# A spectral gate kernel: the last token transform of two row blocks done together on the quarters of the matmul array

## The chip, the cores and the metric

One core of a Trainium2 chip. The metric is the device time of one launch in microseconds (us), the median of the runs. Engines are named as in the profile: PE is the matmul engine (PEld its weight load), DVE the vector engine, ACT the scalar engine, POOL the one that issues the software DMAs, SP the one that issues the hardware DMAs.

## The reference

```python
x = A_x                                        # 1 x 2048 tokens x 512 channels
xn = _layernorm(x, axis=-1)
s = irfft2(rfft2(xn) * (A_w_r + 1j * A_w_i))   # over tokens and channels
h = _layernorm(xn, axis=-1)
u = _gelu(einsum("bsd,sf->bdf", h, B_w1) + B_b1)    # F = 1792
g = _silu((einsum("bdf,fs->bds", u, B_w2) + B_b2).transpose(0, 2, 1))
return x + s * g
```

All data are 32-bit floats. Two branches start from the normalised x: a filter in the two-dimensional frequency domain, and a two-layer network over the tokens whose output gates the filter's result.

## The kernel before

Token t stands at partition t // 16 and in row block j = t % 16, so the 2048 x 512 matrix is 16 row blocks of 128 partitions x 512 channels. The program has three stages.

- **Up to about 100 us**: layer norm of each block, the first products of the network (`hidden_early`), and the first half of the token transform (`first_transform`, `fold`), whose result goes into `ey`, 128 channel pairs x 4 channel groups x 64 frequency columns x 16 blocks x 2.
- **From about 100 to 207 us**: the other network products (`hidden_rest`), gelu, and the filter in eight steps (`filter_pair`), which reads and rewrites `ey`. Two of its matmul groups already run on 64 x 64 quarters of the array: the one that reads `gf` and `sh`, four F32 matmuls with 512 columns each, and the one that reads `xc` and `hf`.
- **From about 207 us to the end**: the second network layer by Strassen-Winograd products, the channel transform back, the last token transform, gate and output. 

In the last stage a loop runs over eight pairs p; a pair is the row blocks j0 = p and j1 = p + 8. Each pair has seven products in the order `ORDER = (1, 2, 5, 6, 3, 7, 4)`; each is 21 matmuls (7 slices of the hidden dimension, each as high x high, high x low, low x high parts; F32R, 128 x 256 columns). Here "product 3" is the one with n = 3. The moving operands are the forms fa, fb, fc, fd of u and the stationary ones are w2f, made for each product by `w2_form`: ACT copies the high part from the loaded weights (L735), DVE subtracts it to get the low part (L736). Three buffers hold w2f, and the form for the product after next is made while PE works. The forms of products 6 and 3 first need a sum of weight blocks (L745 on DVE, `added_up`); each of the sums overwrites the tile `s` that the form before reads, so sum, ACT copy and DVE subtraction follow one another.

Beside the products, each row block j goes through these steps:

- `gathered(j)`: ACT copies block j out of `ey` into `yt` (L807).
- `channels(j, yt)`: four F32 matmuls 128 x 128 (L814; each runs as two passes, so the profile counts eight), then ACT copies one half (L816, `od`), DVE makes sum and difference (L818, L819, `es`) and six more small additions (L821 to L830, `tt` and `y`), and `split` makes a high part `ch` on ACT and a low part `cl` on DVE (L145).
- `spectral(j, y)`: the last token transform, three F32R matmuls of 128 x 512 with the constant `cft` (L148 to L150).
- `gate` (L845, Silu on ACT), `finish` (L853, multiply on DVE) and a DMA. For all blocks but the last the DMA adds into the output, which already holds x (POOL queue, L855); the last block adds x itself (L857) and writes by SP (L858), in two halves of 256 channels.

The products of a pair accumulate in PSUM: products 1, 6, 7 and 4 use the same tile `bx`, and between them ACT or DVE read it (`copied`, `summed`), so product 4 waits until DVE has read `bx` after product 7. In this stage the program orders nothing by hand: the tile scheduler sets the order on each engine, and each engine then runs its queue in that order.

## Time and profile before

| what | value |
|---|---|
| time, median of 3 runs | 380.28 us (380.25 to 381.03) |
| profiled execution: time / span | 380.5 us / 378.7 us |
| granted PE clock, mean | 0.999 |
| PE, DVE, ACT and POOL busy over the span | 98%, 85%, 59%, 20% |
| DMA, last stage (240 to 340 us) | 0.80 to 0.83 of 16 engines busy |

The span is the part of the execution from the first to the last instruction of the program; 1.8 us lie around it. Busy shares are means over stages with different limits, so the prediction reads single stretches of the timeline. In the timeline a row gives the start of the first instruction, the time from there to the end of the last, and how many were merged. Matmuls overlap (one starts while the one before drains), so what a group costs on PE is the distance from its start to the start of the next group, not the second column.

### The profile page before, as it was taken

How to read it: one execution, taken by the hardware profiler on the slowest of the kernel's cores; microseconds unless marked ns; L12 is line 12 of the kernel's file. 1: busy time of each engine (PE TensorE's matmuls, PEld its weight loads, DVE VectorE, ACT ScalarE, POOL GpSimd, SP SyncE). 2: the span in 40 equal slices, each digit the busy share in tenths (PEclk: the TensorE clock that was granted, in tenths of full speed). 3: DMA queues.
4: the chain of work that ended last, by engine and by line, in shares of the span. 5: the costliest groups of instructions: out<-in, count | busy, mean ns of one | idle time of the engine just before them, and what ended most of it. 6: DMA issues, size and time to landing. Idle time of an engine off the chain costs nothing.

```text
span 378.7 us, 7729 instructions
## 1 busy us (share of the span) xinstructions
PE 371.0 (98%) x2872; PEld 326.7 (86%) x2872; DVE 321.6 (85%) x691; ACT 223.7 (59%) x405; POOL 74.5 (20%) x125
## 2 busy tenths in 40 slices
PE   8999999999999999999999899999999999999994
PEld 4888888888877777777888899999999999999994
DVE  5899999985489999999998888897969787987873
ACT  4677867763964444476528685756656465646441
POOL 2133232232222222211111012030302020200100
PEclk9999999999999999999999999999999999999999
DMA  8884778304276475767557289797969696885603
GB/s 257 283 284 147 244 254 275 115 1 126 76 224 216 164 230 188 253 211 234 174 197 158 83 251 212 231 176 198 183 171 222 133 222 133 234 156 153 101 0 55
DMA packets 34101, 68.42 MB, mean 181 GB/s; under 512 B 4352, under 2 KB 17552, under 8 KB 33936
## 3 DMA queue, kind: packets, MB, share of 16 engines
q1 hardware_dynamic: 25712, 43.03, 36.2%
q0 software_dynamic: 8352, 24.91, 29.5%
q8 instruction: 22, 0.36, 0.4%
q14 instruction: 15, 0.12, 0.1%
HBM read 59.53 MB, written 8.13 MB: 179 GB/s over the span
## 4 chain that ended last, share of the span: by engine, by line
PE 86%; DVE 7%; ACT 3%; issue 2%; POOL 0%; DVEq 0%; ACTq 0%; POOLq 0%
PE ps L879 34%; PE ps L134 20%; PE ps L402 20%; PE ps L241 4%; PE ps L814 3%; PE ps L391 2%; PE ps L149 1%; PE ps L148 1%; PE ps L150 1%; ACT w2f L735 1%; DVE w1l L145 1%; DVE fa L307 1%; DVE xc L601 1%; DVE xc L603 1%; DVE w2f L736 1%
## 5 line engine op out<-in xcount | busy, mean ns | idle before, releaser
L402 PE MATMUL ps<-h,w1h 128*128 128x512 f32 x224 | 58.7, 398 | 0.0
L134 PE MATMUL ps<-h,w1h 128*128 128x512 f32 x176 | 56.2, 401 | 0.0
L736 DVE TENSOR_TENSOR w2f<-s,w2f 128x896 fp32r<-128x896 f32 x32 | 34.8, 1092 | 15.6 <-ACT w2f L735 14.9
L402 PEld LDWEIGHTS ps<-h,w1h 128*128 128x128 f32 x224 | 40.9, 188 | 7.9
L879 PE MATMUL ps<-fa,w2f 128*128 128x256 f32 x336 | 43.3, 281 | 0.4 <-DVE w2f L736 0.4
L879 PE MATMUL ps<-fb,w2f 128*128 128x256 f32 x336 | 42.4, 280 | 0.1
L879 PEld LDWEIGHTS ps<-fa,w2f 128*128 128x128 f32 x336 | 41.3, 188 | 1.3 <-DVE w2f L736 0.6
L879 PEld LDWEIGHTS ps<-fb,w2f 128*128 128x128 f32 x336 | 40.5, 188 | 0.7 <-DVE c L849 0.5
L879 PE MATMUL ps<-fc,w2f 128*128 128x256 f32 x336 | 40.9, 279 | 0.0
L134 PEld LDWEIGHTS ps<-h,w1h 128*128 128x128 f32 x176 | 31.6, 188 | 10.7 <-issue 4.9
L879 PEld LDWEIGHTS ps<-fc,w2f 128*128 128x128 f32 x336 | 39.9, 188 | 0.0
L735 ACT ACTIVATE w2f<-s 128x896 fp32r<-128x896 f32 x32 | 30.1, 948 | 15.1 <-DVE s L745 15.1
L726 POOL DMA_DIRECT2D s<-in_w_dram x16 | 14.0, 877 | 108.1 <-DVE es L819 26.8
L134 PE MATMUL ps<-h,w1l 128*128 128x512 f32 x88 | 34.4, 391 | 0.0
L736 DVE TENSOR_TENSOR w2f<-a,w2f 128x896 fp32r<-128x896 f32 x24 | 26.0, 1085 | 5.9 <-ACT w2f L735 5.9
L402 PE MATMUL ps<-h,w1l 128*128 128x512 f32 x112 | 30.6, 389 | 0.0
L735 ACT ACTIVATE w2f<-a 128x896 fp32r<-128x896 f32 x24 | 22.7, 950 | 10.8 <-PE ps L879 7.5
L402 PEld LDWEIGHTS ps<-h,w1l 128*128 128x128 f32 x112 | 21.0, 188 | 4.5
L145 ACT ACTIVATE w1h<-w1s 128x384 fp32r<-128x384 f32 (+1 forms) x26 | 14.6, 566 | 13.8 <-PE ps L134 11.2
L397 DVE TENSOR_TENSOR w1l<-w1r,w1h 128x512 fp32r<-128x512 f32 (+1 forms) x32 | 20.9, 652 | 2.1 <-DMA w1r<-in_w_dram 1.6
L584 POOL DMA_DIRECT2D xc<-xc x16 | 9.8, 619 | 64.3 <-ACT xc L581 54.5
L855 POOL DMA_DIRECT2D out_dram<-g x15 | 13.6, 908 | 43.2 <-DVE g L853 43.2
(119 smaller groups left out, 744.7 us busy)
## 6 DMA issues: line engine op xcount, KB each, us to landing
a<-in_w_dram SPq DMA_DIRECT2D x22, 448.0 KB, 3.8
wt<-in_wk_dram POOLq DMA_DIRECT2D x16, 512.0 KB, 5.4
s<-in_w_dram SPq DMA_DIRECT2D x16, 448.0 KB, 3.8
s<-in_w_dram POOLq DMA_DIRECT2D x16, 448.0 KB, 6.9
w1s<-in_w_dram SPq DMA_DIRECT2D x36, 128.0 KB, 2.6
w1r<-in_w_dram SPq DMA_DIRECT2D x16, 256.0 KB, 3.8
xc<-xc POOLq DMA_DIRECT2D x16, 256.0 KB, 3.0
x<-in_x_dram SPq DMA_DIRECT2D x15, 256.0 KB, 4.3
```

Of the source, the lines that this page charges most:

```text
L134: return lambda *args, **kw: self.keep(operation(*args, **kw))
L145: return A.activation(hi, src, AF.Copy), V.tensor_sub(lo, src, hi.bitcast(F32))
L241: T.matmul(z[:, b], h[:, b * P:(b + 1) * P], c, start=True, stop=True)
L397: keep(V.tensor_sub(dst, src, hi.bitcast(F32)))
L402: T.matmul(ps[:, bank + i], w[wi][:, i * P:(i + 1) * P], hj, start=first and j == 0, stop=last and j == NJ - 1)
L584: keep(G.dma_start(*(v.rearrange("p s t c -> p s (t c)") for v in (there[c::2], here[1 - c::2, ::-1]))))
L726: G.dma_start(t, w2_half(*added), accum_op=ALU.add)
L735: step(A.activation(wf[:, 0], v, AF.Copy))
L736: step(V.tensor_sub(wf[:, 1], v, wf[:, 0].bitcast(F32)))
L814: T.matmul(pe[:, b % 2, b // 2], yt[:, b], ci[:, b], start=True, stop=True)
L855: G.dma_start(out[:, j, cols], g[:, cols], accum_op=ALU.add)
L879: T.matmul(o, wf[:, wi, i], ui, start=m + a == 0 and n in (1, 2, 5), stop=m == NH - 1 and a == 2, skip_group_check=n in (6, 3, 7, 4))
```

## The change

Both row blocks of a pair now go through the channel transform and the last token transform together.

- **Layout.** The symmetry of the last transform is used: a sum and a difference of frequency columns k and 63 - k' are formed in advance, so that even and odd tokens need only 64 of the 128 rows each. `gathered(p)` does it while it copies the pair out of `ey`: two small ACT copies and four DVE additions or subtractions of 240 elements, whose results stand 65 (or 63) elements apart within each pair of values. The tile `yt` has one buffer.
- **`channels(p)`** has the eight F32 matmuls of both blocks; **`unfolded(p)`** has the work behind them on twice the width: one ACT copy of 512 elements, two DVE operations of 512, two of 128, four of 256. The split into `ch` and `cl` is gone.
- **`spectral(p)`**: four F32 matmuls, each 64 x 64 with 512 columns, on the four quarters of the array (rows r, columns e), into PSUM bank e ^ r. They replace the six F32R matmuls of two calls before.
- **Tokens** are permuted: partitions 0 to 63 are the even tokens, 64 to 127 the odd ones. So `w2_form` reads its source with a step of two elements, and the DMAs of xr, b2t and of the output are issued once for each half of the partitions.
- **Order.** Matmuls of the last stage are now held in program order (`T = Kept(...)`, whose line the order shows as L140). `channels(0)` stands behind product 2 of the first pair; `spectral(p)` and `channels(p + 1)` stand between products 7 and 4; for the last pair `spectral` stands behind product 6.
- In the second stage, one ACT copy into `ey` became two; at the start, c_ft is half as large and comes by SP instead of POOL.

```diff
+    b = f.T.reshape(64, 2, P)
+    b = np.concatenate([np.stack([b[0, 0], b[1, 0] + b[1, 1]])[None], b[2:3], b[4:34]]).reshape(64, P)
+    ft = np.concatenate([np.concatenate([b[:, 0::2], b[:, 1::2]], 1)] * 2)
...
-        "c_ft": _parts(f.T, 1),
+        "c_ft": ft.astype(np.float32),
...
-            v = src.rearrange("p (f q) -> p f q", q=P)
-            step(A.activation(wf[:, 0], v, AF.Copy))
-            step(V.tensor_sub(wf[:, 1], v, wf[:, 0].bitcast(F32)))
+            v = src.rearrange("p (f q e) -> p f e q", q=64, e=2)
+            parts = wf.rearrange("p w f (e q) -> p w f e q", e=2)
+            step(A.activation(parts[:, 0], v, AF.Copy))
+            step(V.tensor_sub(parts[:, 1], v, parts[:, 0].bitcast(F32)))
...
+        T = Kept(nc.tensor, keep)
+        halved = (slice(0, 64), slice(0, None, 2)), (slice(64, P), slice(1, None, 2))
...
-        def gathered(j):
-            yt = fp.tile([P, 4, P], F32, name=f"yt{j}", tag="yt", bufs=2)
-            A.activation(yt.rearrange("p b (l c) -> p b l c", c=2), ey[:, :, :, j], AF.Copy)
-            return yt
+        def gathered(p):
+            yt = fp.tile([P, 2, 4, 130], F32, name=f"yt{p}", tag="yt")
+            yts[p] = yt
+            for i, j in enumerate((p, p + NP)):
+                t = yt[:, i]
+                to = t[:, :, :P].rearrange("p b (e s c) -> p b e s c", e=2, c=2)[:, :, ::1 - 2 * i, 0:2]
+                A.activation(to, ey[:, :, 0:4, j].rearrange("p b (e s) c -> p b e s c", e=2), AF.Copy)
+                same = t.rearrange("p b (c t) -> p b t c", c=2)[:, :, 4:64:2]
+                other = t[:, :, 1:127].rearrange("p b (c t) -> p b t c", c=2)[:, :, 4:63:2, ::-1]
+                first, second = (ey[:, :, k, j] for k in (slice(4, 34), slice(63, 33, -1)))
+                yield V.tensor_add((same, other)[i], first, second)
+                yield V.tensor_sub((other, same)[i], first, second)
+
+        def channels(p):
+            yt = yts.pop(p)
+            for i in range(2):
+                pe = ps[:, 6 + i].rearrange("p (h b c) -> p h b c", b=2, c=P)
+                for b in range(4):
+                    T.matmul(pe[:, b % 2, b // 2], yt[:, i, b, :P], ci[:, b], start=True, stop=True)
+
+        def unfolded(p):
+            pe = ps[:, 6:8].rearrange("p i (h k) -> p i h k", h=2)
+            od = fp.tile([P, 2, 256], F32, name=f"od{p}", tag="od")
+            A.activation(od, pe[:, :, 1], AF.Copy)
+            es = fp.tile([P, 2, 2, 2, P], F32, name=f"es{p}", tag="es")
+            V.tensor_add(es[:, :, 0].rearrange("p i b c -> p i (b c)"), pe[:, :, 0], od)
+            V.tensor_sub(es[:, :, 1].rearrange("p i b c -> p i (b c)"), pe[:, :, 0], od)
+            yield
...
+            V.tensor_add(y[:, 0, :, :, 0], ev[:, :, :, 0], ov)
+            V.tensor_sub(y[:, 1, :, :, 0], ev[:, :, :, 0], ov)
+            yield
...
-        def spectral(j, y):
-            mm3(ps[:, j // NP], cft[:, 0], cft[:, 1], *y, True, True)
+        def spectral(p):
+            y = ys.pop(p)
+            for e, cols in enumerate((slice(0, 64), slice(64, P))):
+                for r, rows in enumerate((slice(0, 64), slice(64, P))):
+                    i = e ^ r
+                    T.matmul(ps[cols, i].rearrange("p (s k) -> p s k", s=2), cft[rows, cols], y[rows, :, i], start=True,
+                             stop=True)
...
+            for rows, tokens in halved:
+                if j + 1 < NJ:
+                    G.dma_start(out[tokens, j, cols], g[rows, cols], accum_op=ALU.add)
+                else:
+                    SY.dma_start(out[tokens, j, cols], g[rows, cols])
...
+                    if more:
+                        spectral(p)
+                        run(gathering)
+                        channels(p + 1)
+                        pieces = unfolded(p + 1)
+                        finish(g0, j0, whole)
```

How the built program's order moves, at three places.

First, PE in the middle of the stage: the end of product 7 (the rows that read fb with the first w2f) and the start of product 4 (the next w2f). `ch` and `cl` are the split operand of `spectral`, `yt` is the operand of `channels`, `y` the unsplit operand. Before:

```order
L879 MATMUL ps<-fb_2623,w2f_2_3262 128x256 x3
L148 MATMUL ps<-ch_3308,cft 128x512
L814 MATMUL ps<-cd,yt_3317 128x128
L149 MATMUL ps<-cl_3309,cft 128x512
L150 MATMUL ps<-ch_3308,cft 128x512
L814 MATMUL ps<-cd,yt_3317 128x128 x3
L879 MATMUL ps<-fb_1443,w2f_2_3312 128x256 x3
```

With the change:

```order
L140 MATMUL ps<-fb_2607,w2f_3_3469 128x256 x3
L140 MATMUL ps<-fb_2625,w2f_3_3469 128x256 x3
L140 MATMUL ps<-y_3396,cft 64x512 x4
L140 MATMUL ps<-cd,yt_3399 128x128 x8
L140 MATMUL ps<-fb_1444,w2f_3_3499 128x256 x3
```

Both blocks' channel matmuls and the quarters stand here now; the second `spectral` (behind product 1) and the second `channels` (behind product 6) of each pair are gone from their places.

Second, the entry into the stage. On DVE, the last forms of u (fc, fb), the first sum s, and what comes before the low part of product 6's form (w2f, written from s). Before:

```order
L307 TENSOR_TENSOR fc_2619<-u_2585,fc_2619 128x2x256
L745 TENSOR_TENSOR s_8_2538<-s_8_2538,a_0_2534 128x896
L307 TENSOR_TENSOR fb_2623<-u_2585,fb_2623 128x2x256
L736 TENSOR_TENSOR w2f_0_2687<-s_8_2538,w2f_0_2687 128x896
L849 TENSOR_TENSOR c_0_2718<-ps,p_0_2682 128x256
```

With the change:

```order
L759 TENSOR_TENSOR s_8_2540<-s_8_2540,a_0_2536 128x896
L313 TENSOR_TENSOR fb_2625<-u_2587,fb_2625 128x2x256
L835 TENSOR_TENSOR yt_2639<-ey 128x4x30x2
L836 TENSOR_TENSOR yt_2639<-ey 128x4x30x2 x2
L835 TENSOR_TENSOR yt_2639<-ey 128x4x30x2
L750 TENSOR_TENSOR w2f_0_2671<-s_8_2540,w2f_0_2671 128x896
```

And on PE at the same place, the end of product 2 (fa) and what follows. Before, product 5 (fc with w2f_0_2608) stands ahead of the first channel matmuls:

```order
L879 MATMUL ps<-fa_2612,w2f_0_2548 128x256 x2
L879 MATMUL ps<-fc_1440,w2f_0_2608 128x256
L879 MATMUL ps<-fc_1547,w2f_0_2608 128x256 x3
L879 MATMUL ps<-fc_2290,w2f_0_2608 128x256 x3
L879 MATMUL ps<-fc_2508,w2f_0_2608 128x256 x3
L879 MATMUL ps<-fc_2524,w2f_0_2608 128x256 x3
L879 MATMUL ps<-fc_2602,w2f_0_2608 128x256 x3
L879 MATMUL ps<-fc_2619,w2f_0_2608 128x256 x3
L814 MATMUL ps<-cd,yt_2636 128x128 x4
```

With the change it stands behind them:

```order
L140 MATMUL ps<-fa_2568,w2f_0_2550 128x256 x3
L140 MATMUL ps<-fa_2614,w2f_0_2550 128x256 x3
L140 MATMUL ps<-cd,yt_2639 128x128 x8
L140 MATMUL ps<-fc_1441,w2f_0_2610 128x256 x3
L140 MATMUL ps<-fc_1548,w2f_0_2610 128x256 x3
```

So the first channel matmuls moved ahead of a whole product, and they read a tile that DVE writes late.

Third, DVE from the end of product 4 on: g is the gate of block j1, whose multiplication waits for product 4; s, w2f are the sums and forms of products 5, 6 and 3. Before:

```order
L853 TENSOR_TENSOR g_3168<-ps,g_3168 128x512
L145 TENSOR_TENSOR cl_3393<-y_3387,ch_3392 128x512
L736 TENSOR_TENSOR w2f_3_3425<-s_11_3202,w2f_3_3425 128x896
L745 TENSOR_TENSOR s_11_3202<-s_11_3202,a_3_3205 128x896
L736 TENSOR_TENSOR w2f_3_3455<-s_11_3202,w2f_3_3455 128x896
L849 TENSOR_TENSOR c_3_3486<-ps,p_3_3449 128x256
L745 TENSOR_TENSOR s_11_3202<-s_11_3202,a_3_3237 128x896
L736 TENSOR_TENSOR w2f_3_3490<-s_11_3202,w2f_3_3490 128x896
```

With the change:

```order
L895 TENSOR_TENSOR g_3130<-ps,g_3130 128x512
L863 TENSOR_TENSOR y_3396<-es_3363 128x4x64
L750 TENSOR_TENSOR w2f_3_3368<-s_11_3169,w2f_3_3368 128x896
L867 SCALAR_TENSOR_TENSOR y_3396<-od_3361,es_3363 128x4x64
L759 TENSOR_TENSOR s_11_3169<-s_11_3169,a_3_3172 128x896
L867 SCALAR_TENSOR_TENSOR y_3396<-od_3361,es_3363 128x4x64
L835 TENSOR_TENSOR yt_3399<-ey 128x4x30x2
L750 TENSOR_TENSOR w2f_3_3403<-s_11_3169,w2f_3_3403 128x896
L891 TENSOR_TENSOR c_3_3432<-ps,p_3_3392 128x256
L759 TENSOR_TENSOR s_11_3169<-s_11_3169,a_3_3205 128x896
L750 TENSOR_TENSOR w2f_3_3439<-s_11_3169,w2f_3_3439 128x896
```

The subtraction into cl left this chain, and pieces of y and of the next pair's gather came into it.

108 lines of the change are left out of this document (55 added, 53 removed).

## The prediction

> **What bounds the kernel now.** I read the page's busy shares first (the table above), then the stretch of one pair, then the timeline of single engines. The stretch of one whole pair (columns: its length, busy us and instructions of PE, PEld, DVE, ACT, POOL, then clock, share and GB/s of DMA):
>
> ```profile
> 282.72:303.44 20.72, 20.72 (x173) 20.31 (x171) 16.80 (x32) 12.20 (x21) 3.47 (x4) 1.00 0.79 182
> ```
>
> In the last stage PE is busy all of a pair at full clock; DVE has about 4 us of 20.72 free, ACT 8. So a microsecond of matmul taken out of a pair is worth a microsecond, as long as DVE and ACT still deliver in time. PE's timeline of that pair (product 3 to the next product 3):
>
> ```profile
> 282.72 2.72 PE L879 MATMUL ps<-fa,w2f 128*128 128x256 f32 x21
> 285.28 2.63 PE L879 MATMUL ps<-fb,w2f 128*128 128x256 f32 x21
> 287.75 0.39 PE L148 MATMUL ps<-ch,cft 128*128 128x512 f32 x1
> 287.98 0.38 PE L814 MATMUL ps<-cd,yt 128*128 128x128 f32 x2
> 288.32 0.50 PE L149 MATMUL ps<-cl,cft 128*128 128x512 f32 x1
> ...
> 288.88 0.83 PE L814 MATMUL ps<-cd,yt 128*128 128x128 f32 x6
> 289.47 2.72 PE L879 MATMUL ps<-fb,w2f 128*128 128x256 f32 x21
> 292.02 2.63 PE L879 MATMUL ps<-fd,w2f 128*128 128x256 f32 x21
> 294.50 0.40 PE L148 MATMUL ps<-ch,cft 128*128 128x512 f32 x1
> ...
> 295.20 2.64 PE L879 MATMUL ps<-fa,w2f 128*128 128x256 f32 x21
> ...
> 302.63 1.05 PE L814 MATMUL ps<-cd,yt 128*128 128x128 f32 x8
> 303.44 0.83 PE L879 MATMUL ps<-fa,w2f 128*128 128x256 f32 x5
> ```
>
> By distances of starts: a product is 2.47 us (285.28 to 287.75), or 2.56 right after F32 matmuls (282.72 to 285.28), so that change of kind costs 0.09. One `spectral` alone is 0.70 (294.50 to 295.20), one `channels` 0.81 (302.63 to 303.44). Interleaved, the two take 1.72 (287.75 to 289.47).
>
> **Part 1, PE in a pair: gain.** The quarters are not new. The second stage runs four F32 matmuls of 64 x 64 with 512 columns, eight passes:
>
> ```profile
> 104.53 1.07 PE L134 MATMUL ps<-h,w1e 128*128 128x512 f32 x4
> 105.53 1.09 PE L134 MATMUL ps<-sh,gf 64*64 64x512 f32 x8
> 106.55 0.72 PE L134 MATMUL ps<-h,w1e 128*128 128x512 f32 x2
> ```
>
> They take 1.02 us (105.53 to 106.55). The four matmuls ahead take 1.00, against 4 x 0.23 for such matmuls in the pair (287.75 to 287.98), so entering costs 0.08: 1.10 for a pair's transform. A pair becomes seven products (7 x 2.47 = 17.29), the quarters 1.10, sixteen channel passes (twice 0.81, plus 0.08 as the split group above took 0.93 rather than 0.81: 1.70), and one change back, 0.09: 20.18 instead of 20.72, **0.54 less**. Seven pairs have this form: 3.8 us. In the last pair 2 x 0.70 becomes 1.10 + 0.09, another 0.2. Sum **4.0 us**. Unknown is a change straight from quarters to full-width F32, which no row has; bounds are no cost and the 0.11 by which the first matmul after 106.55 is longer (0.72 for two, against 0.39 + 0.23), 0.8 over all pairs. I take none, since both are F32.
>
> **Part 2, the entry: loss.** PE, DVE and ACT where the stage begins:
>
> ```profile
> 207.17 2.64 PE L879 MATMUL ps<-fd,w2f 128*128 128x256 f32 x21
> ...
> 215.82 1.16 PE L814 MATMUL ps<-cd,yt 128*128 128x128 f32 x8 [1.07 <-ACT yt L807]
> ...
> 220.10 0.48 PE L879 MATMUL ps<-fa,w2f 128*128 128x256 f32 x2
> 220.98 2.27 PE L879 MATMUL ps<-fa,w2f 128*128 128x256 f32 x17 [0.40 <-DVE w2f L736]
> ...
> 214.10 0.69 DVE L307 TENSOR_TENSOR fb<-u,fb 128x512 fp32r<-128x512 f32 x1
> ...
> 214.28 0.95 ACT L735 ACTIVATE w2f<-s 128x896 fp32r<-128x896 f32 x1 [1.30 <-DVE s L745]
> ```
>
> Now, PE has done products 1, 2 and 5 when it waits for the gather, and starts at 215.82. With the change, product 5 stands behind the channel matmuls: products 1 and 2 end at 207.17 + 4.94 = 212.11. The gather stands on DVE behind fb, which leaves the engine at 214.71 (0.61 after its start, the spacing of such operations below). Two of its operations, 0.33 each by the spacing of 256-element ones below, end the engine's turn at 215.37; the third waits for ACT's two small copies, which follow the copy that ends at 215.23, and its result is there about 0.4 later, near 215.8. PE therefore idles 3.7 us instead of 1.07 + 0.64 (220.98 less 220.10 and two matmuls of 0.12). That late low part of product 3's form no longer holds PE up, since product 3 now starts later. Loss **2.0 us**; bounds 1.3 (the third operation doesn't wait and the tile is ready at 215.1) and 3.0 (the gather at twice 0.33).
>
> **Part 3, DVE and ACT in a pair: no cost, with a thin cover.** The rows from the end of product 4 (PE starts product 1 at 292.02):
>
> ```profile
> 290.23 0.42 DVE L818 TENSOR_TENSOR es<-ps,od 128x256 f32<-128x256 f32 x1
> 290.57 0.41 DVE L819 TENSOR_TENSOR es<-ps,od 128x256 f32<-128x256 f32 x1
> ...
> 292.73 0.69 DVE L853 TENSOR_TENSOR g<-ps,g 128x512 f32<-128x512 f32 x1 [0.55 <-ACT g L845]
> 293.34 0.68 DVE L145 TENSOR_TENSOR cl<-y,ch 128x512 fp32r<-128x512 f32 x1
> ...
> 295.22 1.09 DVE L745 TENSOR_TENSOR s<-s,a 128x896 f32<-128x896 f32 x1
> ...
> 296.40 0.95 ACT L735 ACTIVATE w2f<-s 128x896 fp32r<-128x896 f32 x1 [1.32 <-DVE s L745]
> ...
> 297.39 1.09 DVE L736 TENSOR_TENSOR w2f<-s,w2f 128x896 fp32r<-128x896 f32 x1 [1.08 <-ACT w2f L735]
> 298.40 0.42 DVE L849 TENSOR_TENSOR c<-ps,p 128x256 f32<-128x256 f32 x1
> ...
> 300.92 2.20 DVE L736 TENSOR_TENSOR w2f<-s,w2f 128x896 fp32r<-128x896 f32 x2 [1.10 <-ACT w2f L735]
> ```
>
> DVE operations follow each other after 0.34 (256 elements), 0.61 (512) and 1.01 (896). Product 3's form is ready at 302.01 (300.92 + 1.09), needed at 303.44: 1.4 us of slack. With the change PE reaches product 3 without the 0.70 and the 0.81 between: four products after product 4's end, 9.9, or 10.1 for the third matmul, the first to read the low part. The chain on DVE from that end: gate's multiplication from +0.71 to +1.32, a piece of y 0.34, form 5 1.01, a piece 0.34, sum 1.09, ACT 0.09 + 0.95, low part 0.04 + 1.01, c 0.33, sum 1.09, ACT 0.10 + 0.95, low part 0.04 + 1.09, in all +9.8. **Slack 0.3 us**, so the term is nothing, but a chain longer by 0.3 stalls PE each pair. Ahead of it, between the channel matmuls and that multiplication (2.56 + 0.71 = 3.27 us), stand two gather operations, two of 512, a gather, two of 128 (0.2 each) and one of y: 0.67 + 1.22 + 0.33 + 0.4 + 0.34, with 0.1 to start, 3.06. That fits by 0.2.
>
> Whether these durations hold for the new access patterns is the open point. `w2_form` reads with a step of two elements, the gather reads pairs 128 bytes apart and writes single elements 260 bytes apart. Nearest rows, columns as in the page's groups and a line's view:
>
> ```profile
> L807 ACT ACTIVATE yt<-ey x16: 634/691/709, 215.1 to 345.4; 128x512 f32<-128x512 f32 x16
> ...
> L262 DVE SCALAR_TENSOR_TENSOR ey<-t,o x32: 277/284/294, 19.2 to 99.7; 128x128 f32<-128x128 f32 x32
> ...
> L830 DVE SCALAR_TENSOR_TENSOR y<-tt,es 128x128 f32<-128x128 f32 x16 | 4.5, 284 | 0.0
> ...
> 292.60 0.62 ACT L145 ACTIVATE ch<-y 128x512 fp32r<-128x512 f32 x1
> ```
>
> DVE writing scattered pairs (L262) costs what contiguous writing costs, 284 ns both; ACT reading scattered pairs (L807) takes 691 against 620, 11% more. So for the forms I bound the extra cost by nothing and 11%. For DVE's gather the near end is nothing (L262); no row shows single elements written far apart, and the far end, a doubling, is assumed. I take nothing for DVE, as L262 is its nearest row, and a few per cent on ACT, which the slack holds but for some 0.2 us in all at the entry.
>
> [...]
>
> **Part 4, the tail: loss.**
>
> ```profile
> 370.66 0.40 PE L150 MATMUL ps<-ch,cft 128*128 128x512 f32 x1
> ...
> 370.70 0.41 DVE L849 TENSOR_TENSOR c<-ps,p 128x256 f32<-128x256 f32 x1
> ...
> 371.17 2.74 PE L879 MATMUL ps<-fb,w2f 128*128 128x256 f32 x21
> ...
> 372.60 3.10 SPq L858 DMA_DIRECT2D out_dram<-g  x2
> ...
> 374.91 0.42 DVE L857 TENSOR_TENSOR g<-g,xr 128x256 f32<-128x256 f32 x1
> ```
>
> In the last pair product 4 waits until DVE has read what product 7 left; `spectral` covered most of that, leaving 0.28 (371.17 less 370.66 and 0.23). With nothing between, about 0.6 is open (0.41 plus the drain and the signals): 0.3 more. Behind the last addition (375.33) SP issues one DMA, done by 375.70, so 0.37 or less; a second half is another 0.35. Sum **0.65**. The extra DMA issues elsewhere lie in queues with time to spare (POOL: four operations, 3.47 busy of 20.72 us; two more of the like fit). What waits for g's output is the next gate in the same buffer, three products later.
>
> **Sum**: -4.0 + 2.0 + 0.65 = about -1.3; with those 0.2 on ACT I take -1.1. The profiled execution, span 378.7 and 1.8 around it, took 380.5, 0.2 above the median of 380.28; 1.1 less than the median is **379.2**. Its own range, from the bounds: 378.3 to 380.1.
>
> **Rivals.**
>
> - *Slow gather (slower).* Place: DVE ahead of the gate's multiplication and at the entry. Twice the price (0.66 each) adds 1.0 at the entry and 1.0 ahead of that multiplication, 0.8 beyond its 0.2, 0.5 beyond the chain's 0.3; the fourth operation lies in DVE's wait for ACT. Seven pairs lose 0.2 to 0.5 each, with the entry 2.4 to 4.5: 381.6 to 383.7. At one and a half times the slack holds and only the entry's 0.5 is lost: 379.7; it decides from about 1.6 times. For: single elements far apart; against: L262.
> - *Forms late (slower).* The chain holds two ACT copies and three DVE subtractions of forms, 5 us; 11% on all is 0.55, 0.25 beyond the slack, 1.8 over seven pairs: 381. Beyond that each per cent costs 0.35. For: L807; against: only ACT has shown it, and with wider gaps.
> - *Quarters do not run side by side (slower).* Here both row halves write into both banks (bank e ^ r); in the second stage each row half keeps its own bank. If two of four must wait, 1.02 becomes 2.04, eight times: 387. The rows at 105.53 do not decide it. [...] No run before shows two row halves on one bank, and the two that share one here write different partitions.
> - *Better.* The scheduler's waits at the entry are worth less than reckoned, because what PE waits for there DVE would have owed it later: the 2.0 shrinks to 0.5, 377.7.
>
> **How the numbers follow.** Forecast 0.47, slow gather 0.20, late forms 0.14, banks 0.06, better 0.13. What a measurement can tell from no change is about 0.2%, 0.76 us: faster means below 379.5. The forecast gives 0.37 of its 0.47 to that, and with the better case faster is 0.50; no change 0.15 (the forecast's upper end and the milder of the slow gather); slower 0.35. The range 377.7 to 382.4 leaves out the banks, the worst of the late forms and a little below.
>
> **What would show it.** Right: a pair of about 20.2 us from product 3 to product 3, a quarter group of eight passes in 1.0 to 1.1, a wait of 3 to 4 us on PE at the first channel matmuls, no wait at product 3. Wrong: gather operations well over 0.41 each or forms over 1.09 and 0.95, with PE waiting for w2f at product 3 in each pair; quarters that take 2 us.

## The result, and the profile after

The changed kernel takes 385.5 us (median, 384.63 to 386.61), the kernel before beside it 380.46 us (380.25 to 381.03): a ratio of 1.0132 (95% interval 1.0099 to 1.0164). In a second set it was 1.0105 (1.0089 to 1.0120). It is slower by about one per cent; 379.2 us, 1.1 us faster, was forecast. The profiled execution took 384.9 us with a span of 382.9, against 380.5 and 378.7.

Both kernels reach product 7 of a pair with the channel transforms of that pair behind them, so its starts cut the stage into pieces. PE's timeline of the kernel before (product 1 of the first pair, then product 7 of the second, third and seventh pair):

```profile
207.17 2.64 PE L879 MATMUL ps<-fd,w2f 128*128 128x256 f32 x21
...
244.31 2.63 PE L879 MATMUL ps<-fb,w2f 128*128 128x256 f32 x21
...
264.75 2.63 PE L879 MATMUL ps<-fb,w2f 128*128 128x256 f32 x21
...
347.22 2.63 PE L879 MATMUL ps<-fb,w2f 128*128 128x256 f32 x21
```

The same of the changed kernel, with product 7 of the second to the fifth and the seventh pair (tile `fb`), and product 1 of two of them between (tile `fd`):

```profile
206.79 2.64 PE L140 MATMUL ps<-fd,w2f 128*128 128x256 f32 x21
...
247.57 2.63 PE L140 MATMUL ps<-fb,w2f 128*128 128x256 f32 x21
...
268.10 2.63 PE L140 MATMUL ps<-fb,w2f 128*128 128x256 f32 x21
...
275.96 2.54 PE L140 MATMUL ps<-fd,w2f 128*128 128x256 f32 x21
...
288.64 2.63 PE L140 MATMUL ps<-fb,w2f 128*128 128x256 f32 x21
...
296.59 2.64 PE L140 MATMUL ps<-fd,w2f 128*128 128x256 f32 x21
...
309.17 2.63 PE L140 MATMUL ps<-fb,w2f 128*128 128x256 f32 x21
...
350.24 2.63 PE L140 MATMUL ps<-fb,w2f 128*128 128x256 f32 x21
```

| piece | before | after | difference | forecast |
|---|---|---|---|---|
| start of the span to product 1 | 207.17 | 206.79 | -0.38 | 0 |
| product 1 to the second pair's product 7 | 37.14 | 40.78 | +3.64 | +1.7 (entry +2.0, ACT's copies there +0.2, a pair -0.54) |
| five pairs, product 7 to product 7 | 102.91 | 102.67 | -0.24 | -2.7 (5 x 0.54) |
| the seventh pair's product 7 to the end of the span | 31.48 | 32.66 | +1.18 | -0.1 (a pair -0.54, last transform -0.2, tail +0.65) |
| span | 378.7 | 382.9 | +4.2 | -1.1 |

By each of these product 7s the kernel before has transformed one row block more than the changed one, which is worth 0.5 us by the quarters below; so the entry cost some 4.1 us (3.64 and 0.5) and the end some 0.7 (1.18 less 0.5).

Two things are to be seen. The loss is at the entry. And the pairs gained nothing: 20.53 us each against 20.58. The changed kernel's pairs are moreover all alike, 20.53 to 20.54, although PE's products are not: product 1 at 275.96 is 0.1 us shorter than that at 296.59, and so are all the four from product 1 to product 6 of that pair, while the two pairs around them last 20.54 and 20.53. A pair that stays the same when PE is faster is not held by PE.

**The entry.** PE's timeline of the changed kernel (product 2, the first channel matmuls, products 5 and 6, product 3; then the first quarters and the next pair's channel matmuls):

```profile
209.27 2.63 PE L140 MATMUL ps<-fa,w2f 128*128 128x256 f32 x21
216.09 2.94 PE L140 MATMUL ps<-cd,yt 128*128 128x128 f32 x16 [4.19 <-DVE yt L836]
218.68 6.00 PE L140 MATMUL ps<-fc,w2f 128*128 128x256 f32 x42
224.52 2.63 PE L140 MATMUL ps<-fa,w2f 128*128 128x256 f32 x21
...
229.56 1.09 PE L140 MATMUL ps<-y,cft 64*64 64x512 f32 x8
230.57 2.05 PE L140 MATMUL ps<-cd,yt 128*128 128x128 f32 x16
```

Product 2 ends at 211.74, so PE waits 4.35 us for the gather. Then the sixteen channel passes take 2.59 us (216.09 to 218.68), where the next pair's take 1.81 (230.57 to 232.38, the start of product 4), and products 5 and 6 take 5.84, though a product takes 2.47, or 2.56 behind F32 matmuls. The stretches of that time (length, then busy us and instructions of PE, PEld, DVE, ACT, POOL, granted clock, share and GB/s of DMA) say why:

```profile
212.00:216.00 4.00, 0.00 (x0) 0.00 (x0) 3.76 (x8) 2.68 (x7) 0.00 (x0) 1.00 0.18 46
216.00:220.00 4.00, 3.91 (x22) 3.91 (x23) 3.65 (x8) 2.67 (x4) 0.00 (x0) 0.63 1.03 348
220.00:225.00 5.00, 5.00 (x43) 5.00 (x43) 5.00 (x11) 2.19 (x7) 0.86 (x1) 0.95 0.87 239
```

The granted clock is 0.63 behind the wait. The shares of DMA are high there too, so the clock alone is not yet shown to be the cause.

**A pair.** The quarters take 1.01 us (229.56 to 230.57) and 1.02 to 1.03 in the later pairs, as forecast. DVE's timeline of one pair, from the end of the channel matmuls (PE starts product 4 at 294.03, product 1 at 296.59) to product 3's form:

```profile
294.31 0.62 DVE L835 TENSOR_TENSOR yt<-ey 128x240 f32<-128x240 f32 x1 [0.18 <-PE ps L140]
294.76 0.61 DVE L836 TENSOR_TENSOR yt<-ey 128x240 f32<-128x240 f32 x1
295.22 0.68 DVE L853 TENSOR_TENSOR es<-ps,od 128x512 f32<-128x512 f32 x1
...
296.41 0.60 DVE L836 TENSOR_TENSOR yt<-ey 128x240 f32<-128x240 f32 x1
...
297.58 0.68 DVE L895 TENSOR_TENSOR g<-ps,g 128x512 f32<-128x512 f32 x1
...
303.44 1.08 DVE L759 TENSOR_TENSOR s<-s,a 128x896 f32<-128x896 f32 x1
305.68 2.29 DVE L750 TENSOR_TENSOR w2f<-s,w2f 128x896 fp32r<-128x896 f32 x2 [1.16 <-ACT w2f L749]
```

Product 3's low part is ready at 306.77 (305.68 and 1.09 for the first of the two). PE starts product 3 at 306.48 and its third matmul, 0.23 later, has to wait: the product takes 2.69 us (306.48 to 309.17) instead of 2.47. The chain of waits, which in the kernel before runs through PE alone from the first product 3 (220.98) to the last product, now leaves PE on the way to product 3 in three of the pairs, those in which PE's products are the shorter ones. Its last pieces ahead of one of these, with the matmuls that it then returns to (start, length, engine, tile, line):

```profile
324.06 1.01 DVE s L759
325.17 1.02 ACT w2f L749
326.22 1.10 DVE w2f L750
327.36 8.00 PE ps L140 x64
```

### The profile page after: what moved, and what is told of

Read it like the earlier page. It is cut to its first block, busy times and chain, and to the rows that moved or that the text cites. A ratio compares the mean times of both kernels' runs of the same rounds, so it can differ in the third digit from the quotient of the medians.

```text
span 382.9 us, 7730 instructions
## 1 busy us (share of the span) xinstructions
PE 370.4 (97%) x2888; PEld 321.1 (84%) x2888; DVE 322.4 (84%) x643; ACT 211.1 (55%) x382; POOL 86.2 (23%) x139
## 4 chain that ended last, share of the span: by engine, by line
PE 86%; DVE 9%; ACT 3%; issue 1%; POOL 0%; ACTq 0%; POOLq 0%
PE ps L140 61%; PE ps L408 20%; PE ps L247 4%; DVE w2f L750 3%; DVE s L759 2%; ACT w2f L749 2%; PE ps L397 1%; DVE yt L836 1%; DVE yt L835 1%; DVE g L895 1%; DVE es L854 0%; DVE es L853 0%; DVE c L891 0%; DVE y L862 0%; DVE y L863 0%
## 5 line engine op out<-in xcount | busy, mean ns | idle before, releaser
L140 PE MATMUL ps<-h,w1h 128*128 128x512 f32 x176 | 56.2, 400 | 0.0
L140 PE MATMUL ps<-fa,w2f 128*128 128x256 f32 x336 | 43.6, 281 | 1.1 <-DVE w2f L750 1.1
L140 PEld LDWEIGHTS ps<-fa,w2f 128*128 128x128 f32 x336 | 40.7, 188 | 3.0 <-DVE w2f L750 2.2
L140 PE MATMUL ps<-fb,w2f 128*128 128x256 f32 x336 | 42.5, 280 | 0.6 <-DVE c L891 0.6
L749 ACT ACTIVATE w2f<-s 128x896 fp32r<-128x896 f32 x32 | 32.8, 1026 | 15.5 <-DVE s L759 15.5
L140 PE MATMUL ps<-fc,w2f 128*128 128x256 f32 x336 | 41.2, 282 | 0.0
L140 PEld LDWEIGHTS ps<-fb,w2f 128*128 128x128 f32 x336 | 40.3, 188 | 0.8 <-issue 0.8
L140 PEld LDWEIGHTS ps<-h,w1h 128*128 128x128 f32 x176 | 31.6, 188 | 10.7 <-issue 4.9
L140 PEld LDWEIGHTS ps<-fc,w2f 128*128 128x128 f32 x336 | 40.4, 191 | 0.0
L750 DVE TENSOR_TENSOR w2f<-a,w2f 128x896 fp32r<-128x896 f32 x24 | 26.1, 1092 | 11.3 <-ACT w2f L749 10.6
L140 PE MATMUL ps<-h,w1l 128*128 128x512 f32 x88 | 34.4, 391 | 0.0
L749 ACT ACTIVATE w2f<-a 128x896 fp32r<-128x896 f32 x24 | 24.8, 1038 | 16.8 <-PE ps L140 9.1
L900 POOL DMA_DIRECT2D out_dram<-g x30 | 25.2, 983 | 36.7 <-DVE g L895 30.7
L140 PEld LDWEIGHTS ps<-cd,yt 128*128 128x128 f32 x128 | 15.7, 200 | 10.1 <-issue 5.7
```

Of the source, the lines that this page charges most:

```text
L140: return lambda *args, **kw: self.keep(operation(*args, **kw))
L749: step(A.activation(parts[:, 0], v, AF.Copy))
L750: step(V.tensor_sub(parts[:, 1], v, parts[:, 0].bitcast(F32)))
L900: G.dma_start(out[tokens, j, cols], g[rows, cols], accum_op=ALU.add)
```

## The experiments

The theory after this reading had three parts: (A) at the entry a longer wait on PE and, because of it, a lower granted clock; (B) in the pairs a loop from product 3 through PE to the channel matmuls' end, then through DVE and ACT back to product 3's form, which is longer than PE's own work; (C) more DMA issues at the end. All were edited from the changed kernel. All ratios are to the kernel before, on the same chip. "To the second pair" is the distance in the profile from product 1 to the second pair's product 7, "pair" the mean of the five distances from there to the seventh pair's product 7. By the first of these places the kernel before has transformed a row block more, 0.5 us, which counts when another row of that column is set beside its own.

| kernel | ratio (95%) | to the second pair | pair |
|---|---|---|---|
| before | 1 | 37.14 | 20.58 |
| changed | 1.0132 (1.0099 to 1.0164) | 40.78 | 20.53 |
| changed, again | 1.0105 (1.0089 to 1.0120) | 40.72 | 20.56 |
| first channels behind product 5 | 1.0023 (1.0013 to 1.0034) | 37.95 | 20.55 |
| wait filled | 1.0058 (1.0044 to 1.0073) | 39.26 | 20.54 |
| w2 laid out | 1.0075 (1.0051 to 1.0099) | 41.20 | 20.41 |
| near reads | 1.0080 (1.0063 to 1.0097) | 40.66 | 20.45 |
| moved gather | 1.0096 (1.0078 to 1.0114) | 42.31 | 20.31 |
| output layout | 1.0070 (1.0058 to 1.0083) | 40.91 | 20.51 |
| all four | 0.9988 (0.9976 to 1.0000) | 38.34 | 20.25 |
| all four, quick entry with GpSimd | 0.9989 (0.9980 to 0.9998) | 38.95 | 20.31 |
| all four, quick entry | 0.9967 (0.9953 to 0.9980) | 38.05 | 20.22 |
| the same, gather behind y | 0.9952 (0.9938 to 0.9965) | 37.54 | 20.31 |

**First channels behind product 5.** In the loop's first pass, under `n == 5` instead of `n == 2`:

```diff
                 elif n == 5:
                     p5 = copied(f"p5_{p}", bz)
+                    if p == 0:
+                        channels(p)
+                        pieces = unfolded(p)
...
                 elif n == 2:
                     gate(g0, j0, left_, summed(f"c11_{p}", by, p1), 1.0)
-                    if p == 0:
-                        channels(p)
-                        pieces = unfolded(p)
```

> Only the place of the first channel transform changes: behind product 5 of the first pair (as in the kernel before) instead of behind product 2. Theory (the entry costs 4.8 us: 3.3 of a longer wait on PE, 1.6 because the granted clock falls behind that wait): products 1, 2 and 5 end 2.47 us later than 1 and 2 do, so the wait shrinks from 4.35 to about 1.9 us, the granted clock stays at 1.0, channels take 1.8 instead of 2.6 and the products next to them 2.5 instead of 3.4; from product 1 to product 3 of the first pair about 14 us instead of 17.7; 3 to 3.7 us less than the changed kernel, 381.8 to 382.5. Rival (the slow products at the entry are contention with the weights' DMAs or something else at that place, not the clock): channels and the product behind them stay slow, only the 2.5 us of the wait come off, about 383. Second rival (what PE waits for at the entry DVE owes it later anyway, as the forecast's better case had it): product 6 or 3 then waits for its form, under 1.5 us less, over 384.

Its timeline of PE, and the stretch that had the clock of 0.63:

```profile
211.59 2.63 PE L140 MATMUL ps<-fc,w2f 128*128 128x256 f32 x21
215.92 2.05 PE L140 MATMUL ps<-cd,yt 128*128 128x128 f32 x16 [1.70 <-DVE yt L836]
...
220.20 0.39 PE L140 MATMUL ps<-fa,w2f 128*128 128x256 f32 x2
```

```profile
216.00:220.00 4.00, 4.00 (x36) 4.00 (x37) 3.86 (x7) 3.01 (x4) 0.00 (x0) 1.00 1.04 319
```

The wait is 1.86 us, the granted clock behind it 1.00, the channels and product 6 behind them take 4.28 (to 220.20; 1.81 and 2.47 at full clock), and from product 1 (206.64) to product 3 it is 13.56 us instead of 17.73. The ratio falls by 0.8 to 1.1%. The first rival falls, since the products at that place are fast; the second falls as well, though a part comes back: product 3 waits 0.5 us, and the first quarters 0.8 for the last piece of y, which DVE makes late. The single edit removes most of the loss.

**Wait filled.** Ahead of the first channel matmuls:

```diff
+                        for _ in range(16):
+                            T.matmul(ps[:, 0], hs_fill[0], hs_fill[1], start=True, stop=True)
                         channels(p)
```

`hs_fill` holds 128 and 512 columns of `fa`, a form that is ready by then.

> Sixteen matmuls of 128x512 that nothing reads (into a free bank, about 3.7 us) stand ahead of the first channel transform, where PE idles 4.35 us; nothing else changes. Theory (the granted clock falls because PE idles that long): the filled PE begins the channels at the same time as before, within 0.2 us, but at the full clock: channels 1.8 instead of 2.6, product 5 2.5 instead of 3.4, 1.4 to 1.7 us less than the changed kernel, about 383.9. Rival (those products are slow for another reason: DMA traffic, or the change from one kind of matmul to another): no change, within 0.4 us.

PE's timeline, and the stretch that had the clock of 0.63:

```profile
211.77 3.80 PE L140 MATMUL ps<-fa 128*128 128x512 f32 x16
216.22 2.05 PE L140 MATMUL ps<-cd,yt 128*128 128x128 f32 x16 [0.66 <-DVE yt L836]
218.03 5.19 PE L140 MATMUL ps<-fc,w2f 128*128 128x256 f32 x42
```

```profile
216.00:220.00 4.00, 3.78 (x32) 3.78 (x33) 4.00 (x8) 3.17 (x4) 0.00 (x0) 1.00 0.99 313
```

The channel matmuls start no sooner (9.4 us after product 1, 9.3 before), the DMA engines are about as busy (a share of 0.99 from 216 to 220, against 1.03), and the clock is 1.00: channels 1.81, products 5 and 6 together 5.03 instead of 5.84. To the second pair it is 1.5 us less, and the ratio falls by 0.5 to 0.7%. Nothing was done for these microseconds but to keep PE from idling. So of the entry's loss 1.5 to 1.6 us is the granted clock, which falls behind an idle stretch of 4.35 us and not behind the 1.07 of the kernel before or the 1.86 of the variant above (1.00 from 216 to 220 in both). In other variants that idle about as long, 4.12 us with w2 laid out and 3.87 with the moved gather, the price was higher: the same two groups, channels and product 5, take 6.8 and 7.0 us there, against 6.0 in the changed kernel and 4.4 at full clock, and the granted clock from 216 to 220 is 0.50 in both, against 0.63. So in these runs 3.87 to 4.35 us of idle PE brought the clock down, and 1.07 and 1.86 did not. Why waits of nearly the same length differ in price is not shown.

**w2 laid out.** The host puts the even tokens of w2 ahead of the odd ones, so the forms read contiguously:

```diff
-            v = src.rearrange("p (f q e) -> p f e q", q=64, e=2)
-            parts = wf.rearrange("p w f (e q) -> p w f e q", e=2)
-            step(A.activation(parts[:, 0], v, AF.Copy))
+            v = src.rearrange("p (f q) -> p f q", q=P)
+            step(A.activation(wf[:, 0], v, AF.Copy))
...
-        "w2": w2.reshape(NF, P, P, NJ).transpose(3, 1, 0, 2).reshape(NJ, P, NF * P),
+        "w2": w2.reshape(NF, P, P // 2, 2, NJ).transpose(4, 1, 0, 3, 2).reshape(NJ, P, NF * P),
```

> Only the layout of w2 in DRAM changes: the host puts the even tokens of each block ahead of the odd ones, so that the forms are made with contiguous reads, as in the kernel before. Theory (the pairs are held by the chain sum, ACT's copy, DVE's low part ahead of product 3, two copies of which cost 0.08 us more through the reads with a step of two): ACT's high part falls from 1.03 to 0.95, the low part stays at 1.09, product 3 waits 0.15 less in each pair where it waited, 1 to 1.5 us less than the changed kernel, about 384. Rival (the gather alone holds the chain; ACT has room): high part 0.95, waits as before, under 0.4 us less.

ACT's high part by groups, first of the changed kernel, then of this one (count, busy us and mean ns of one):

```profile
L749 ACT ACTIVATE w2f<-s 128x896 fp32r<-128x896 f32 x28 | 28.7, 1025 | 13.7 <-DVE s L759 13.7
```

```profile
L748 ACT ACTIVATE w2f<-s 128x896 fp32r<-128x896 f32 x28 | 26.6, 949 | 13.5 <-DVE s L758 13.5
```

1025 ns become 949, DVE's low part stays (1090 ns, then 1092), and a pair falls from 20.53 to 20.41, 0.12, close to the two copies that lie on the loop (0.15). The rival falls. The profile's pairs make 0.8 us; the ratio's interval is too wide to say more.

**Tried patterns.** A second operation of 240 elements behind each of the gather's four, on a scratch tile:

```diff
+                at = tr.rearrange("p b (c t) -> p b t c", c=2)[:, :, 4:64:2]
+                run_of = tr[:, :, :60].rearrange("p b (t c) -> p b t c", c=2)
+                flat = ey.rearrange("p b l j c -> p b (l j) c")
...
+                    yield V.tensor_add(run_of, first, second)
...
+                    yield V.tensor_add(at, flat[:, :, 0:30], flat[:, :, 32:62])
...
+                    yield V.tensor_sub(at, first, ey[:, :, 34:64, j])
...
+                    yield V.tensor_sub(*(v.rearrange("p b t c -> p b c t") for v in (at, first, second)))
```

> Behind each of the gather's four operations stands a second one of the same 240 elements on a scratch tile that nothing reads, to be timed by itself: the same reads with contiguous writes; contiguous reads with the gather's writes (pairs, 16 bytes apart); the gather's reads without the reversal and the same writes; and the gather's pattern with the two channels outermost, so that each inner step moves 128 bytes in the reads and 16 bytes in the writes. [...] If the far reads cost: the first 0.61, the second 0.41. If only the reversal costs: the third 0.41 and the first 0.61. The time of the whole says nothing, since DVE has 2.5 us more to do in a pair (about 390 or more).

The groups of DVE, in this order: one of the gather's own, contiguous writes, contiguous reads, no reversal, channels outermost:

```profile
L839 DVE TENSOR_TENSOR yt<-ey 128x240 f32<-128x240 f32 x13 | 8.1, 625 | 0.8 <-PE ps L140 0.8
...
L841 DVE TENSOR_TENSOR tr<-ey 128x240 f32<-128x240 f32 x6 | 2.5, 422 | 0.0
...
L843 DVE TENSOR_TENSOR tr<-ey 128x240 f32<-128x240 f32 x6 | 3.6, 608 | 0.2
...
L846 DVE TENSOR_TENSOR tr<-ey 128x240 f32<-128x240 f32 x6 | 3.7, 615 | 0.1
...
L848 DVE TENSOR_TENSOR tr<-ey 128x240 f32<-128x240 f32 x7 | 4.6, 650 | 0.1
```

In the first four the writes cost, not the reads. (The expectation describes the writes wrongly: they are single elements, the two of a pair 260 bytes apart in the scratch tile, 260 or 252 in the gather's own.) Reading scattered pairs and writing contiguously takes 422 ns, about what the kernel's contiguous operations of 256 elements take (0.41 to 0.42 us). Single elements written far apart take 608 to 625 with each of the three reads tried. With the channels outermost the writes come every 8 bytes, but the reads are then single elements 128 bytes apart: 650; which of the two costs there is not shown. For single elements written far apart the prediction had no row; here they have a figure, 1.44 to 1.48 times the 422 ns for 240 elements, and 1.54 times with the channels outermost. The forms' reads with a step of two cost DVE's low part nothing that can be seen (1090 ns with them, 1092 without), while ACT's copy took 8% longer with them (1025 ns against 949).

**Near reads.** The gather reads neighbouring elements instead of the transform's tokens; so other values go through the last transform:

```diff
-                first, second = (ey[:, :, k, j] for k in (slice(4, 34), slice(63, 33, -1)))
+                flat = ey.rearrange("p b l j c -> p b (l j) c")
+                first, second = flat[:, :, 0:30], flat[:, :, 32:62]
```

> The gather's four operations read elements that lie next to each other in the same tile instead of the channel transform's tokens (so other values go through the last transform); count, sizes, writes and everything else stay. Theory (from product 3 to product 3 a pair of the changed kernel is held by a loop in which DVE's and ACT's work from the channel matmuls to product 3's form is the long part, and three of the four gather operations lie on it): operations 0.42 us instead of 0.615, one after another at 0.33 instead of 0.44, the loop 0.1 to 0.3 shorter, pairs 20.25 to 20.45 instead of 20.54, the wait at product 3 smaller by as much; at the entry some 0.4 of PE's 4.35 us less; in all 1.2 to 2.5 us less. Rival (the gather is covered and the forms' reads with a step of two alone hold product 3): operations as fast, pairs as before, only the entry's 0.4 us.

A miss: it took the reads for the cost, which the rows above already spoke against. The operations stay at 609 and 614 ns, so the edit does not make them cheap. What the pairs show about the loop, they show without it: the four of 20.42 to 20.45 are those in which product 3 or product 7 is one of the faster products (the quarters follow product 7 after 2.48 and 2.47 us at 267.85 and 308.72, after 2.56 elsewhere; product 3, its wait included, takes 2.60 and 2.61 at 265.25 and 306.11, where the changed kernel's takes 2.69), and the fifth, with neither, is 20.52. The run with the output layout, whose gather is unchanged, has the same: 20.45 and 20.46 in its two such pairs, 20.53 to 20.56 in the others. Products 3 and 7 lie on the loop, between the form and the channel matmuls; where only products 1, 2, 5 and 6 are faster, as in the changed kernel, the pair stays. The ratio's fall against the changed kernel, 0.25 to 0.5%, is little more than what two sets of that kernel differ by.

**Moved gather.** A second buffer for `yt`, and the four operations pinned just ahead of low parts for which DVE waits on ACT anyway:

```diff
-            yt = fp.tile([P, 2, 4, 130], F32, name=f"yt{p}", tag="yt")
+            yt = fp.tile([P, 2, 4, 130], F32, name=f"yt{p}", tag="yt", bufs=2)
...
             step(A.activation(parts[:, 0], v, AF.Copy))
+            between(name)
             step(V.tensor_sub(parts[:, 1], v, parts[:, 0].bitcast(F32)))
...
+        SLOTS = ({}, {"7_0": 2, "4_0": 2}, {"5_1": 1, "6_1": 1, "3_1": 1, "7_1": 1})
+        for q in range(1, NP):
+            where = SLOTS[q] if q < 3 else {f"1_{q - 1}": 1, f"2_{q - 1}": 1, f"6_{q - 1}": 1, f"3_{q - 1}": 1}
```

> The gather's tile gets a second buffer, and from the third pair's on the four operations stand where DVE waits for ACT anyway (just ahead of the low parts of the forms 1, 2, 6 and 3, a pair earlier) instead of between the channel matmuls and product 3's form; the second pair's stand ahead of the low parts of 7 and 4. Nothing else changes, the entry's order included. Theory (the loop through DVE holds the pairs, not PE): the loop is 0.4 to 0.7 us shorter and PE becomes the bound: no wait over 0.15 us at product 3, pairs of 20.2 to 20.35 (less where the products take 2.38 us each), 1.3 to 3 us less than the changed kernel. Rival (product 3 waits for the sum, ACT's copy and the low part by themselves, whatever stands ahead): pairs 20.5 as before, within 0.5 us.

The stretch of one pair, product 3 to product 3 (columns as above):

```profile
267.78:288.09 20.31, 20.31 (x173) 19.37 (x172) 17.17 (x27) 10.53 (x18) 5.14 (x6) 1.00 0.80 186
```

Product 3 waits no more, and every pair from the third on is 20.31: the loop held the pairs, and without it PE does. No work has gone; its place has changed, and the tile has a second buffer, which that place needs (the two were not tried apart). The time was missed, though. It is 42.31 us to the second pair instead of 40.78, because the slow clock lasted longer (1.1 us) and the pinned order makes product 3 of the second pair wait 0.34 us ahead of its first matmul and 0.73 ahead of its third. The gain of the pairs is given back there.

**Output layout.** Even rows ahead of odd ones in DRAM, whole DMAs again:

```diff
-            for rows, tokens in halved:
-                if j + 1 < NJ:
-                    G.dma_start(out[tokens, j, cols], g[rows, cols], accum_op=ALU.add)
-                else:
-                    SY.dma_start(out[tokens, j, cols], g[rows, cols])
+            if j + 1 < NJ:
+                G.dma_start(out[:, j, cols], g[:, cols], accum_op=ALU.add)
+            else:
+                SY.dma_start(out[:, j, cols], g[:, cols])
```

> The output lies in DRAM with the even rows ahead of the odd ones (the copy of x into it writes it so, the host puts it in order), so that each piece of the output is one DMA again instead of two. Theory (the tail's second issue costs 0.35 to 0.5, and POOL's fifteen extra issues cost nothing): 0.3 to 0.6 us less than the changed kernel, from the end of the last product to the end about 5.1 instead of 5.6. Rival (the extra issues also hold up the weights' second halves, which POOL issues too, and with them product 3): pairs shorter by 0.1 or more, 1 us or more in all. Second rival: no change, the two last DMAs go side by side.

SP's DMAs at the end, first of the changed kernel, then of this one:

```profile
376.18 3.93 SPq L902 DMA_DIRECT2D out_dram<-g  x4
```

```profile
376.05 3.08 SPq L902 DMA_DIRECT2D out_dram<-g  x2
```

From the last product's start to the end of the span it is 6.99 us (381.7 less 374.71) instead of 8.06 (382.9 less 374.84): 1.07 less, of which 0.99 lies behind the start of the last addition (3.36 us, 381.7 less 378.34, instead of 4.35). That is about twice what was expected. The pairs are as before within 0.1, so the fifteen extra issues on POOL cost nothing that can be seen; the cost is the tail's.

**All four at once.** First channels behind product 5, w2 laid out, moved gather and output layout together.

> All of it at once: first channel transform behind product 5, w2 laid out on the host, gather with two buffers in DVE's waits, output with even rows ahead. Theory: 3.1 us from the entry, 2 to 3 in the pairs (PE-bound, where the layout of w2 adds little to the moved gather), 0.4 in the tail: 5.5 to 6.5 us less than the changed kernel, some 379 to 380 where the kernel before takes 380.5 to 381.5, a ratio of 0.994 to 0.998 to it. Rival (a loop through ACT or a DMA comes next and holds the pairs near 20.4): 381, no better than the kernel before.

380.63 us against 381.34: the loss is gone, but the ratio, 0.9988, is no gain that can be told. The pairs are PE's in the three of 20.31 to 20.32. In the two of 20.16 and 20.17, with products of 2.38 us, product 3 waits 0.3 again: a loop is left that is hardly shorter than PE's 20.31. Missing is the entry, 38.34 us against 37.14, to which the 0.5 of the row block is to be added: PE waits 1.2 us for the gather and 2.1 for product 3's form, 1.1 for its high part and 1.0 for its low part, since the load of the gate's table (1.28 us) had come to stand ahead of that copy on ACT.

**The changed kernel again.**

> The changed kernel itself once more, beside the kernel before and the two variants of this set, so that differences of a few tenths are taken on one chip: a ratio of 1.010 to 1.016 to the kernel before, a second profile with the wait of about 4.3 us at the first channel matmuls, a lower granted clock behind it and pairs of 20.5 us on the mean. If the loop through DVE holds the pairs, their sum from the first product 3 to the seventh is 122.3 to 123 again, whichever pairs have products of 2.38 us and whichever 2.47. If PE held them it would move with those.

It is 1.0105, with 40.72 us to the second pair (40.78 in the first profile) and the same mean granted clock over the span, 0.993. From the first product 3 to the seventh it is 123.09, just past the range. Pairs by product 7 are 20.54 to 20.57, though the products of 2.38 us stand in other pairs than in the first profile: it is the loop, not PE's whole work, that sets them.

**Quick entry, with GpSimd and without.** From the kernel with all four:

```diff
+            if name == "6_0":
+                t = fp.tile([P, 1], F32, name="early")
+                keep(A.activation(t, b2t[:, :1], AF.Silu))
...
-        SLOTS = ({}, {"7_0": 2, "4_0": 2}, {"5_1": 1, "6_1": 1, "3_1": 1, "7_1": 1})
+        SLOTS = ({}, {"4_0": 4}, {"5_1": 1, "6_1": 1, "3_1": 1, "7_1": 1})
```

and, in the first of the two alone:

```diff
-        added_up(cur["s1"], cur["a12"])
+        keep(G.tensor_add(cur["s1"], cur["s1"], cur["a12"]))
```

> As the kernel with all four parts, and three more at the entry: the sum ahead of the first form 6 on GpSimd, which is idle there, instead of on DVE; the table of the gate's function loaded by a one-element operation while ACT waits; the second pair's gather behind the first y. Theory (with the pairs bound by PE what is left is DVE's backlog at the entry, where PE waits 1.2 us for the gather, 1.0 for form 6 and 1.0 for form 3, and 0.5 in the next pair): a microsecond less on DVE and 1.3 on ACT ahead of those, 1.5 to 2.5 us less than the kernel with all four parts, a ratio of about 0.993 to 0.996 to the kernel before. Rival (GpSimd's sum is slow or slows DVE beside it, and form 6 comes later still): no gain, a wait of 2 us or more at product 6.

> As the kernel before in this list, but with the first sum on DVE as it was. Theory: the early table and the later gather bring form 3's 1.0 us, the gather's 1.2 and form 6's 1.0 stay: 0.7 to 1.2 us less than the kernel with all four parts. If GpSimd's sum is what helps, this one is 0.8 to 1.3 us slower than the one with it; if it harms, this one is the faster.

GpSimd's sum harms: 0.9989 against 0.9967, and 0.9 us more to the second pair. The wait of 2 us at product 6 that the rival spoke of did not come; the first channel matmuls already start 0.9 us later (9.52 us behind product 1, not 8.61). The row of POOL, and those of DVE beside it:

```profile
209.37 2.12 POOL L820 TENSOR_TENSOR s<-s,a 128x896 f32<-128x896 f32 x1 [7.92 <-DVE w2f L761]
```

```profile
208.19 1.09 DVE L761 TENSOR_TENSOR w2f<-s,w2f 128x896 fp32r<-128x896 f32 x1
209.43 2.61 DVE L313 TENSOR_TENSOR fa<-u,fa 128x512 fp32r<-128x512 f32 x1
```

DVE's operation, 0.69 us in the run without GpSimd's sum, takes 2.61: it ends at 212.04, 0.55 behind the end of POOL's (211.49), so by an estimate from these ends it hardly moved until POOL's was over. (The expectation speaks of form 6 and form 3; both waits were product 3's.) Without it the ratio is 0.2%, or 0.8 us, below that of all four, as expected; their intervals just overlap, though, and only 0.3 of it stands in the profile up to the second pair.

**Gather behind y.** `SLOTS` has `{"1_1": 4}` for the second pair.

> As the variant with the first sum on DVE and the early table, but the second pair's four gather operations stand behind the whole y of the first pair instead of ahead of its last piece, just ahead of the low part of the next pair's form 1. Theory (what is left at the entry is the order on DVE: the first pair's last transform waits 0.9 us for y's last piece, which stands behind 1.8 us of gather): that wait is gone, the gather fills DVE's wait of 0.75 us for ACT, product 3 of the second pair waits no more than before: 0.7 to 1.3 us less than that variant, a ratio of 0.993 to 0.996 to the kernel before. Rival (DVE's backlog comes back a little later whatever the order): the next channel matmuls or the second pair's product 3 wait longer by as much, no gain.

379.57 us against 381.3, 0.9952: faster than both kernels. The first pair's last transform waits no more, and it is 37.54 us to the second pair, 0.5 less; product 3 of the second pair still waits 0.74 us, as the rival had it in part. The intervals of this and the variant above overlap, so the last step's gain is read from the profile, not from the times.

## Why the prediction was wrong

Two steps failed: part 3 put DVE and ACT in a pair at nothing, and they took most of what PE gained there; part 2 left out the clock. By the table above, the profile lies 5.3 us above the forecast (+4.2 against -1.1). The five pairs have 2.5 of it, a little less than half by part 3 and the rest by the sizes of part 1. With the row block counted where it belongs, the entry has 2.5, of which the clock is 1.6, and the end 0.8.

**Part 1, PE in a pair.** The quarters were right (1.02 us), so the rival with the banks falls. From 229.65 to 229.75 four of the eight passes are under way at once, and by the order of the matmuls these are the four quarters, so two row halves with different partitions of one bank were under way together, and the group took 1.01 us, not the rival's 2.04. One size was off: the new pair is 20.31 where PE alone holds it, not 20.18; of that 0.11 is the sixteen channel passes, 1.81 instead of 1.70. And the old pair was read from one stretch, 20.72, the longest of five whose mean is 20.58, since some products in the others take 0.09 us less. Against that stretch PE alone gains 0.41 a pair, against the mean 0.27, half of the 0.54.

**Part 3, "slack 0.3 us, so the term is nothing".** This step cost what was left of the gain in the pairs: 0.22 of the 0.27 us (20.53 instead of PE's 20.31). From product 4's end to product 3's low part it is 10.18 us (296.59 to 306.77), not 9.8. The multiplication of the gate comes at +0.99 instead of +0.71, because the three gather operations ahead of it follow each other after 0.44 us instead of 0.33 and the first starts 0.28 behind the channel matmuls, not 0.1: what "fits by 0.2" did not fit. ACT's two copies are 0.07 longer each. Together some 0.4, over a slack of 0.3. By the prediction's own slack each of the two rivals was there at a price at which it alone would have done nothing (the gather at 1.33 times its spacing, where 1.6 was the point; the copies at 8%, where 0.3 us was the room), and they lie on one chain. The runs bear that out for the copies: with the gather moved a pair is PE's 20.31. The gather alone, with w2 laid out, still holds the pair 0.1 above that (20.41), so its room was smaller than reckoned.

**Part 2, the entry.** The wait was mis-sized within its bounds: 4.35 us instead of 3.7. PE waits for the third of the gather's operations on DVE:

```profile
214.56 0.59 DVE L835 TENSOR_TENSOR yt<-ey 128x240 f32<-128x240 f32 x1
214.99 1.05 DVE L836 TENSOR_TENSOR yt<-ey 128x240 f32<-128x240 f32 x2
```

Two of them take 0.11 more to the next and the third itself 0.2 more, 0.4 in all; the rest is that PE reaches this place 0.37 earlier (211.74 instead of 212.11) and DVE only 0.15. What was missing is the clock: 1.5 to 1.6 us, shown by filling the wait. A forecast of 3.7 us of idle PE should have asked what the clock does behind it.

**Part 4, the tail.** Both terms had the right sign and were too small. PE and DVE at the end of the changed kernel:

```profile
371.69 2.54 PE L140 MATMUL ps<-fb,w2f 128*128 128x256 f32 x21
...
374.84 2.71 PE L140 MATMUL ps<-fb,w2f 128*128 128x256 f32 x21 [0.61 <-DVE c L891]
...
378.55 0.42 DVE L897 TENSOR_TENSOR g<-g,xr 128x256 f32<-128x256 f32 x1
```

Product 7 is one of 2.38 us here, so ahead of the last product PE waits 0.77 us (374.84 less 371.69 and 2.38) instead of 0.28 (forecast +0.3); from the last addition's start to the end of the span it is 4.35 us (382.9 less 378.55) instead of 3.79, 0.56 more (forecast 0.35).

**Better.** What PE waits for at the entry DVE did owe in part: of the 2.5 us that the first variant took off the wait, 1.3 came back a little later, and the other variants have such waits too (0.5 to 1.1 us each). But in the changed kernel the wait alone cost 2.6 us more than the waits of the kernel before (4.35 less 1.71), and the clock came on top; the 0.5 of this case did not come.

## What to carry to other kernels

Where a slack is smaller than the sum of what is unknown on its chain, add the unknowns of all rivals before calling the term nothing; here two, of which one was too small alone and the other nearly so, ate most of the gain. Measure an old period over many repeats and look whether it moves with the engine that is thought to bound it. And where an edit lets PE idle for several microseconds, price the clock behind the wait too, or fill the wait: here 4.35 us of idle PE brought the granted clock to 0.63 over the next 4 us, which cost 1.5 to 1.6 us.

## What the runs showed that was not expected

Products of 21 matmuls take 2.47 us in some pairs and 2.38 in others, in most of the profiles, that of the kernel before included (with the gather moved and with it behind y none is faster), at a granted clock of 1.00 in both; what sets it stays open. A DVE operation with two inputs in SBUF took 2.61 us instead of 0.69 beside a GpSimd operation of 2.12 us: in this one row the price, 1.92 us, is nearly the whole of the other's time.
